# Indirect scatters planned one by one behind a wait on ScalarE or VectorE, and keys times values per head

## The chip, the core and the metric

The kernel runs on one core of a Trainium2 chip. The core has a matrix engine (TensorE, "PE" in the profile; its weight loads are "PEld"), VectorE ("DVE"), ScalarE ("ACT"), GpSimd ("POOL") and SyncE ("SP"). Each takes its own instructions in order and waits for the others on semaphores. Sixteen DMA engines move data between the chip's memory and the core; SP, ACT and POOL can each issue transfers. The metric is the device time of one execution in microseconds (us), given as the median of several runs; lower is better.

## What is computed

A linear attention block is followed by a mixture of eight experts in which each token goes to two of them. Cut to what matters:

```python
# attention: 4 batches, 4 heads, 1088 tokens, head size 32, r = 8
a, b = x @ S1.T, x @ S2.T                 # for queries and for keys
phi = outer(a, b)                         # 64 features a head
kv  = einsum('bhsf,bhsd->bhfd', phi_k, v) # keys times values
z   = phi_k.sum(over tokens)
x   = (phi_q @ kv) / (phi_q @ z + 1e-6)   # 4352 tokens of 128
# router and experts
noisy = x @ w_gate + log1p(exp(x @ w_noise)) * noise
top2, weights = the two largest of 8 and their softmax
out[token] = sum over the two: weight * (relu(x @ w1[e]) @ w2[e])
```

All of it is float32. The hidden size of an expert is 1024.

## The kernel before

The work goes batch by batch through the attention, and in waves through the experts. The tokens of a batch lie in nine chunks: eight of 128 rows, and a last one of 64.

*Attention of a batch* (`keys_values`, L626, and `queries`). VectorE transposes the keys and queries, TensorE multiplies them with the sketch, ScalarE or VectorE copies the result, and VectorE forms the products of features (`features`, L566). POOL copies the values into `vaug` (L629 and L632), a tile with 64 columns a head: 32 of values, one of ones (so that the sum z comes out of the same matmul) and 31 of zeros. TensorE multiplies features by values in L653: per chunk two matmuls, each with two heads side by side as weights (128 columns) and as moving data (128 columns). Only the two blocks on the diagonal, each head with itself, are used. They are copied out to `kvT` and folded with the gate weights (L674). `queries` transposes the query features (L698), multiplies by the folded matrix (L709), and divides.

*Router* (`router`). VectorE and ScalarE find each token's two experts, their weights and a place in the expert's list. For each chunk and each of the two choices POOL then issues one indirect scatter (L794) that writes up to 128 weighted rows from `xg` into the lists `xs` in the chip's memory. The first four chunks of batch 0 are wave 0 (8 scatters), the rest of batch 0 is wave 1 (10), and batches 1 to 3 are waves 2 to 4 (18 each).

*Experts* (`block`). A block is one expert with 128 rows (waves 0, 1 and the last, static one) or 256 rows (waves 2 to 4). Its rows are fetched from `xs` once the scatters of its wave and of the one before have landed. Then TensorE multiplies by w1 (L1054), ScalarE or VectorE applies the relu (L1062 or L1060), TensorE multiplies by w2 (L1069), the result is copied to `y` (L310), and POOL scatters `y` into `pairs` (L794 again), one scatter per 128 rows. Later `sums` reads both rows of every token from `pairs`, adds them and writes the output.

*The order of all this.* A planner written out in the kernel (class `Plan`) takes every piece of work as a job with engines, a cost, a priority and its dependencies. `order` (L92) gives each a planned start by a greedy simulation of the queues, and `write` (L153) emits the instructions in that order; each engine then runs its own in order. Jobs marked `paced` are the scatters of rows from wave 1 on and all the scatters of results. Among the paced ones, the fifth after another may start no sooner than 7.0 us after it (`BURST`, `SPAN`), in planned time. Nothing holds the chip to the planned times: only true dependencies are waited for.

*The memset.* Ahead of each indirect scatter, `pool_scatter` clears one element of a small tile on POOL (L793). Nothing else uses that tile.

Of the kernel before, what the change touches and what calls it, by code (L numbers as in the profile page):

```python
# [8 lines left out]
F32 = mybir.dt.float32  # L9
# [27 lines left out]
class Plan:  # L37
# [4 lines left out]
    RATE = 290e3  # L42
    SLACK = 0.35
    LANES = 8
    BURST, SPAN = 5, 7.0
    SOON = 0.3
    AHEAD = 6.0

# [38 lines left out]
    def order(self):  # L87
        free, done, moved, paced, lanes = {}, [], 0.0, [], []
        left = {j: len(j.deps) for j in self.jobs}
        after = {j: [] for j in self.jobs}  # L90
        for j in self.jobs:
            for d in j.deps:  # L92
                after[d].append(j)
        cand = [j for j in self.jobs if not left[j]]
        number = {j: i for i, j in enumerate(self.jobs)}

        def ready(j, e):

            slack = self.SLACK if e == "PE" else 0.0
            return max((d.end if d.engine == e and d.size is None else d.done + slack for d in j.deps), default=0.0)  # L100

        while cand:
            starts = []
            for j in cand:
                at = 0.0
                for b in j.opens:
                    bufs, _, used = self.tags[b.tag]
                    if b.placed or len(used) < bufs:
                        continue
                    ends = [x.done for x in used[-bufs].users]  # L110
                    if None in ends:
                        at = None
                        break
                    at = max(at, max(ends))
                if at is None:
                    continue
                if j.size is not None:
                    if "SP" in j.engines:
                        at = max(at, moved - self.AHEAD)
                    if "POOL" not in j.engines and len(lanes) >= self.LANES:  # L120
                        at = max(at, lanes[-self.LANES])
                if j.paced and len(paced) >= self.BURST:
                    at = max(at, paced[-self.BURST] + self.SPAN)
                for e in j.engines:
                    starts.append((max(at, free.get(e, 0.0), ready(j, e)), j, e))
            assert starts, [(j.engines, j.prio, [b.tag for b in j.opens]) for j in cand]
            first = min(x[0] for x in starts)
            _, s, _, j, e = min((j.prio, s, number[j], j, e) for s, j, e in starts if s <= first + self.SOON)
            cand.remove(j)
            cost = j.cost[e] if isinstance(j.cost, dict) else j.cost  # L130
            j.start, j.end, j.engine = s, s + cost, e
            free[e] = j.end
            if j.paced:
                paced.append(s)
            j.done = j.end + j.lat + self.SYNC
            if j.size is not None:
                moved = max(moved, j.end + 0.6) + j.size / self.RATE
                j.done = max(j.done, moved + 0.8 if e == "SP" else j.end + 1.4 + 2 * j.size / self.RATE)
                if e != "POOL":
                    lanes.append(j.done)  # L140
            j.opens = [b for b in j.opens if not b.placed]
            for b in j.opens:
                b.placed = True
                self.tags[b.tag][2].append(b)
            done.append(j)
            for a in after[j]:
                left[a] -= 1
                if not left[a]:
                    cand.append(a)
        assert len(done) == len(self.jobs)  # L150
        return done

    def write(self, idle=None):  # L153
        last = 0.0
        for j in self.order():
            if idle is not None and "PE" in j.engine:
                idle(last, j.start)
                last = j.end
            for b in j.opens:
                b.t = self.tags[b.tag][1]()  # L160
            j.emit(j.engine)


@with_exitstack
def kernel(
# [122 lines left out]
    def vec(n):  # L288
        return 0.155 + 0.00104 * n
# [4 lines left out]
    def gps(n):  # L294
        return 0.12 + 0.00092 * n
# [4 lines left out]
    def mm(n):  # L300
        return max(0.205, 0.016 + 0.00162 * n)
# [5 lines left out]
        return {"ACT": act(n), "DVE": vec(n)}  # L307

    def copy(e, o, i):
        A.copy(o, i) if e == "ACT" else V.tensor_copy(o, i)  # L310

    def dma(q, o, i, r, w, prio, size=0, issue=0.45, after=(), done=None):

# [82 lines left out]
    starts = const.tile([P, NW + 1, E], F32, name="starts")  # L396
    stops = const.tile([P, NW, E], F32, name="stops")
    over = const.tile([P, E], F32, name="over")
    vaug = const.tile([P, C + 1, H, 2 * DH], F32, name="vaug")
    phk = const.tile([P, C + 1, H, R * R], F32, name="phk")  # L400
    phq = const.tile([P, C + 1, H, R * R], F32, name="phq")
    kvws = [const.tile([P, 2, 2 * YW], F32, name=f"kvw{i}") for i in range(2)]
# [7 lines left out]
    def pool_job(cost, prio, emit, w, r=()):  # L410
        add("POOL", cost, lambda e: emit(), r=r, w=w, prio=prio)

    def constants():
# [152 lines left out]
    def features(jobs, prio, whole=False, after=(), first=None):  # L566


        ps = new("bank")
# [39 lines left out]
        while i < n:  # L609
            m = i  # L610
            while m < n and m - i < 2 and jobs[m][2] is jobs[i][2]:
                m += 1

            def product(e, i=i, m=m):
                shape = [rows.stop, H * (m - i), R, R]
                V.tensor_tensor(  # L616
                    out=jobs[i][2].t[rows, jobs[i][1]:jobs[m - 1][1] + 1, :, :].rearrange("p c h (i j) -> p (c h) i j", i=R),
                    in0=factors(i, m, 0).unsqueeze(3).to_broadcast(shape),
                    in1=factors(i, m, 1).unsqueeze(2).to_broadcast(shape), op=ALU.mult)
            add("DVE", vec(256 * (m - i)), product, r=list(source), w=[(jobs[i][2], jobs[x][1]) for x in range(i, m)], prio=prio)  # L620
            i = m
        return last

# [2 lines left out]
    def keys_values(b, prio, head=False, after=()):  # L626
        kT, qT, pk, pq, va = new("kT"), new("qT"), new("phk"), new("phq"), new("vaug")
        kld, qld, vld = klds[b], qlds[b], vlds[b]
        pool_job(gps(1024), prio, lambda: G.tensor_copy(  # L629
            va.t[:, 0:C, :, 0:DH].rearrange("p c h d -> p h c d"), vld.t[:, :, 0:C, :]), [(va, 0)],  # L630
            ["ones_v"] + [(vld, l) for l in range(4)])
        pool_job(gps(128), prio, lambda: G.tensor_copy(va.t[0:HB, C, :, 0:DH], vld.t[0:HB, :, C, :]), [(va, 1)],  # L632
                 ["ones_v", (vld, 4), (vld, 5)])
# [13 lines left out]
        for ts in ((0, 1), (2, 3), (4, 5), (6, 7), (8,)) if head else (range(C + 1),):  # L647
            def emit(e, ts=ts):
                for t in ts:
                    K = HB if t == C else P  # L650
                    for a in range(2):
                        hs = slice(2 * a, 2 * a + 2)
                        T.matmul(kvp.t[:, P * a:P * a + P], lhsT=va.t[0:K, t, hs, :].rearrange("p h d -> p (h d)"),  # L653
                                 rhs=pk.t[0:K, t, hs, :].rearrange("p h f -> p (h f)"),
                                 start=(t == 0 and a == 0), stop=(t == C), skip_group_check=True)
            add("PE", 2 * len(ts) * mm(P), emit, lat=0.15, w=[kvp], prio=prio + 3.5,
                r=[(pk, t) for t in ts] + [(va, 0), (va, 1)])
        kvT, kvw = new("kvT"), new("kvw")
        kv_of[b] = (kvw, pq)

        def rows_of(l):
            return slice(64 * l, 64 * l + DH + 1)

        for l in range(2):
            add(EV, either(128), lambda e, l=l: copy(
                e, kvT.t[rows_of(l), :, :],
                kvp.t[rows_of(l), 0:2 * P].rearrange("p (a f) -> p a f", a=2)[:, :, 64 * l:64 * l + 64]),
                r=[kvp], w=[(kvT, l)], prio=prio + 3)
        ps = new("bank")

# [119 lines left out]

    def pool_scatter(**kw):

        G.memset(step[:, 0:1], 0.0)  # L793
        return G.indirect_dma_start(**kw)  # L794

    onehot = {}
# [203 lines left out]
    def block(u, w, e, r, n):  # L1000
# [48 lines left out]
        for g in range(FJ // js):  # L1049
# [7 lines left out]

            def relu(en, hp=hp, h=h):
                if en == "DVE":
                    V.tensor_scalar_max(h.t[:], hp.t[:], 0.0)  # L1060
                else:
                    A.activation(out=h.t[:], in_=hp.t[:], func=AF.Relu)  # L1062
            add(EV, either(512), relu, r=[hp], w=[h], prio=TOP + u)

            def second(_, g=g, h=h):
# [245 lines left out]
```

## Time and profile before

| | us |
|---|---|
| median of 3 runs | 407.78 (405.43 to 415.69) |
| the profiled execution, its own time | 410.3 |
| its span in the trace | 408.5 |
| PE busy / PEld busy | 355.0 / 326.7 |
| POOL busy | 179.9 |
| DVE busy / ACT busy | 153.2 / 137.4 |

The mean clock granted to TensorE over the profiled execution was 0.936 of full speed. The profile lists busy times, a strip of 40 equal slices of the span in which a digit is the busy share in tenths, groups of instructions by line, and who waited for whom. In a row of the timeline stand the start, the duration, the engine, the line, the operation with what it writes and reads, how many instructions are merged, and in brackets the idle time before with what ended it. "issue" means that the profile shows nothing that was waited for, and "remote" that the wait was ended by no instruction of the trace. A matmul in float32 leaves two records. The duration that a record shows overlaps with the next, so the rate is read from starts.

### The profile page before, as it was taken

Reading aid. Unit: us, or ns where it says so; the run is one execution under the profiler, and the core shown is the slowest. Engines: PE = TensorE matmul, PEld = TensorE weight load, DVE = VectorE, ACT = ScalarE, POOL = GpSimd, SP = SyncE. Lnnn points to the kernel's source line nnn. Section 1 sums busy time; section 2 is a strip of 40 time slices with the busy share of each in tenths; the row PEclk is TensorE's granted clock in tenths of the full one; section 3 lists DMA queues with packets and bytes.
Section 4 is the critical chain, followed back from the end, with each engine's and each line's share of the span. In section 5 each row is a group of like instructions: output and inputs, shape, how many; then the busy total and the mean of one; then the engine's idle time right before and its main releaser. Section 6 shows DMA issues by size and latency. Waiting matters only on the chain.

```text
span 408.5 us, 7355 instructions
## 1 busy us (share of the span) xinstructions
PE 355.0 (87%) x2563; PEld 326.7 (80%) x2565; DVE 153.2 (37%) x584; ACT 137.4 (34%) x283; POOL 179.9 (44%) x377
## 2 busy tenths in 40 slices
PE   7989669699998698539999998899999999999960
PEld 4759659599997597529997978799999999999960
DVE  6797638268866379204881000110001110001201
ACT  2253233136423153003533332334333434344320
POOL 7827406641377636850346658124232332324320
PEclk9999898979999979957999999899999999999995
DMA  6999993322511106610142322541121521114503
GB/s 168 275 313 348 247 205 83 100 45 39 116 46 40 42 11 94 102 36 0 19 65 54 64 60 60 126 106 38 36 43 32 156 70 26 34 26 126 144 18 88
DMA packets 66969, 37.80 MB, mean 93 GB/s; under 512 B 48911, under 2 KB 59697, under 8 KB 66928
## 3 DMA queue, kind: packets, MB, share of 16 engines
q1 hardware_dynamic: 61488, 27.33, 29.8%
q0 software_dynamic: 4800, 9.29, 7.0%
q10 hardware_dynamic: 640, 0.67, 0.6%
q8 instruction: 21, 0.34, 0.4%
q14 instruction: 20, 0.16, 0.1%
HBM read 24.24 MB, written 13.29 MB: 92 GB/s over the span
## 4 chain that ended last, share of the span: by engine, by line
issue 37%; POOL 27%; PE 19%; DMA 9%; DVE 5%; POOLq 1%; ACT 1%; SPq 0%; ACTq 0%; DVEq 0%
POOL pairs L794 13%; POOL xs L794 10%; PE acc L1069 5%; PE hp L1054 5%; PE bank L582 3%; DMA ix<-xs 3%; PE bank L653 2%; POOL step L793 2%; DMA vld<-in_v_dram 2%; PE bank L709 2%; DMA x<-in_moe_noise_dram 2%; DMA xs<-xg,to 1%; PE bank L698 1%; DMA pairs<-y,mine 1%; POOL xb L317 1%
## 5 line engine op out<-in xcount | busy, mean ns | idle before, releaser
L1069 PE MATMUL acc<-w2s,h 128*128 128x128 f32 x1152 | 156.1, 281 | 8.7 <-ACT h L1062 8.6
L1069 PEld LDWEIGHTS acc<-w2s,h 128*128 128x128 f32 x1152 | 150.1, 196 | 16.0 <-ACT h L1062 10.7
L1054 PE MATMUL hp<-bT,w1s 128*128 128x128 f32 (+1 forms) x768 | 150.2, 330 | 1.8 <-DVE lim L943 1.8
L794 POOL DMA_INDIRECT pairs<-y,mine x72 | 71.3, 990 | 176.7 <-ACT y L310 153.0
L1062 ACT ACTIVATE h<-hp 128x512 f32<-128x512 f32 x139 | 82.7, 597 | 158.8 <-PE hp L1054 97.8
L1054 PEld LDWEIGHTS hp<-bT,w1s 128*128 128x128 f32 x768 | 113.2, 193 | 8.0 <-issue 2.4
L794 POOL DMA_INDIRECT xs<-xg,to x72 | 71.7, 996 | 27.4 <-issue 21.7
L1044 DVE STREAM_TRANSPOSE bT<-xb 128x256 f32<-128x256 f32 (+1 forms) x40 | 15.6, 390 | 152.0 <-PE hp L1054 95.1
L653 PE MATMUL bank<-phk,vaug 128*128 128x128 f32 (+1 forms) x108 | 17.6, 302 | 11.8 <-issue 11.8
L653 PEld LDWEIGHTS bank<-phk,vaug 128*128 128x128 f32 (+1 forms) x108 | 15.2, 208 | 14.0 <-issue 13.7
L310 ACT COPY y<-acc 128x128 f32<-128x128 f32 (+1 forms) x48 | 15.3, 319 | 31.0 <-PE acc L1069 21.8
L709 PE MATMUL bank<-kvw,pT 128*128 128x98 f32 x144 | 18.9, 276 | 3.7 <-ACT pT L310 3.2
L1102 DVE TENSOR_TENSOR o<-pr 128x512 f32<-128x512 f32 (+2 forms) x12 | 6.8, 567 | 40.5 <-DMA pr<-pairs 38.8
L709 PEld LDWEIGHTS bank<-kvw,pT 128*128 128x128 f32 x144 | 17.5, 192 | 5.2 <-ACT pT L310 3.4
L582 PE MATMUL bank<-sk,kT 128*128 128x128 f32 (+1 forms) x72 | 13.1, 339 | 3.9 <-issue 3.6
L582 PE MATMUL bank<-sk,qT 128*128 128x128 f32 (+1 forms) x72 | 13.6, 327 | 3.2 <-issue 2.1
L310 ACT COPY pT<-bank 128x512 f32<-128x512 f32 (+1 forms) x20 | 10.6, 543 | 15.6 <-PE bank L698 10.2
L582 PEld LDWEIGHTS bank<-sk,kT 128*128 128x128 f32 (+1 forms) x72 | 10.9, 233 | 5.4 <-issue 4.3
L582 PEld LDWEIGHTS bank<-sk,qT 128*128 128x128 f32 (+1 forms) x72 | 11.2, 221 | 4.6 <-issue 3.8
L310 ACT COPY lo<-bank 128x256 f32<-128x256 f32 (+2 forms) x21 | 7.1, 337 | 18.7 <-PE bank L582 14.1
L616 DVE TENSOR_TENSOR phk<-ab 128x512 f32<-128x512 f32 (+1 forms) x20 | 13.2, 680 | 0.3
L793 POOL MEMSET step<- 1x1 f32 x144 | 12.7, 88 | 0.0
(158 smaller groups left out, 247.7 us busy)
## 6 DMA issues: line engine op xcount, KB each, us to landing
w1s<-in_moe_w_dram SPq DMA_DIRECT2D x8, 512.0 KB
w2s<-in_moe_w_dram SPq DMA_DIRECT2D x8, 512.0 KB
xb<-xs SPq DMA_DIRECT2D x96, 32.0 KB
pr<-pairs SPq DMA_DIRECT2D x6, 512.0 KB
kq<-in_k_dram SPq DMA_DIRECT2D x4, 544.0 KB
kq<-in_q_dram SPq DMA_DIRECT2D x4, 544.0 KB
vld<-in_v_dram SPq DMA_DIRECT2D x14, 128.0 KB
out_dram<-o SPq DMA_DIRECT2D x6, 256.0 KB
```

The source lines that it names most:

```text
L310: A.copy(o, i) if e == "ACT" else V.tensor_copy(o, i)
L582: T.matmul(ps.t[rows, 2 * W * i:2 * W * i + 2 * W], lhsT=lhsT, rhs=sk[:].rearrange("p c h x -> p (c h x)"), start=True, stop=True)
L616: V.tensor_tensor(out=jobs[i][2].t[rows, jobs[i][1]:jobs[m - 1][1] + 1, :, :].rearrange("p c h (i j) -> p (c h) i j", i=R), in0=factors(i, ...
L653: T.matmul(kvp.t[:, P * a:P * a + P], lhsT=va.t[0:K, t, hs, :].rearrange("p h d -> p (h d)"), rhs=pk.t[0:K, t, hs, :].rearrange("p h f -> ...
L709: T.matmul(ps2.t[:, c0:c0 + 2 * YW], lhsT=pT.t[:, P * (2 * i + a):P * (2 * i + a) + P], rhs=kvw.t[:, a, :], start=True, stop=True)
L793: G.memset(step[:, 0:1], 0.0)
L794: return G.indirect_dma_start(**kw)
L1044: add("DVE", vec(P * n), lambda _: V.transpose(bT.t[:, 0:P * n], flat()), r=[xb], w=[bT], prio=TOP + u)
L1054: T.matmul(hp.t[:, P * n * i:P * n * (i + 1)], lhsT=w1s[:, e, P * (js * g + i):P * (js * g + i + 1)], rhs=bT.t[:, 0:P * n], start=True, st ...
L1062: A.activation(out=h.t[:], in_=hp.t[:], func=AF.Relu)
L1069: T.matmul(acc.t[:, D * c:D * c + D], lhsT=h.t[:, P * (n * i + c):P * (n * i + c + 1)], rhs=w2s[:, e, j, :], start=(j == 0 and c == 0), st ...
L1102: add("DVE", vec(P * c), lambda e, t=t, o=o, rows=rows, c=c: V.tensor_tensor(out=o.t[rows, 0:c, :], in0=t.t[rows, 0:c, 0, :], in1=t.t[rows ...
```

## The change

There are four parts.

1. *Planned one by one.* `BURST, SPAN = 5, 7.0` becomes `GAP = 1.7`. A paced scatter starts, in planned time, at least 1.7 us after the one before it. The eight scatters of wave 0 are counted among those before, though not held back themselves.
2. *The memset waits.* While writing, `write` notes each single instruction of ACT or DVE with its planned end. For a paced scatter it takes, of those whose planned end is not after the scatter's planned start, the one that ends last (`anchor`), and the memset ahead of the scatter gets a real dependency on it. To make this possible, `copy` and `relu` return their instruction. The unpaced scatters of wave 0 have no such dependency.
3. *Keys times values per head.* `vaug` has 33 columns a head, and the memset of its zeros goes. Each chunk has four matmuls, one a head, with 33 columns of weights and 64 of moving data, where it had two with 128 and 128. The result has 128 columns, where it had 256. The planner's cost a chunk goes from two times `mm(128)`, 0.446, to 0.35.
4. *Copies of the values.* The one copy of eight chunks becomes two, of two heads each; the copy of the last chunk stays. In batch 0 the three run on ACT, in the other batches on POOL as before, with a priority later by 0.5.

The product of features gets a list of engines that holds only DVE and a cost for each of two engines; with that list nothing changes in it.

```diff
-    BURST, SPAN = 5, 7.0
+    GAP = 1.7
...
-                if j.paced and len(paced) >= self.BURST:
-                    at = max(at, paced[-self.BURST] + self.SPAN)
+                if j.paced and paced:
+                    at = max(at, paced[-1] + self.GAP)
...
-            if j.paced:
+            if j.paced or "POOL" in j.engines and j.cost == 1.3:
                 paced.append(s)
...
-        last = 0.0
+        last, seen = 0.0, []
...
-            j.emit(j.engine)
+            self.anchor = max((x for x in seen if x[0] <= j.start), default=(0, 0, None))[2] if j.paced else None
+            ins = j.emit(j.engine)
+            if j.engine in ("ACT", "DVE") and hasattr(ins, "ins"):
+                seen.append((j.end, len(seen), ins))
...
-    vaug = const.tile([P, C + 1, H, 2 * DH], F32, name="vaug")
+    vaug = const.tile([P, C + 1, H, DH + 1], F32, name="vaug")
...
-        pool_job(1.2, 4, lambda: G.memset(vaug[:, :, :, DH:2 * DH], 0.0), ["ones_v"])
...
+        by = ("ACT",) if head else ("POOL",)
...
+        for h in range(0, H, 2):
+            add(by, {"ACT": act(512), "POOL": gps(512)}, lambda e, h=h: v_copy(
+                e, va.t[:, 0:C, h:h + 2, 0:DH].rearrange("p c h d -> p h c d"), vld.t[:, h:h + 2, 0:C, :]),
+                w=[(va, h)], r=["ones_v"] + [(vld, l) for l in range(4)], prio=prio + 0.5)
+        add(by, {"ACT": act(128), "POOL": gps(128)}, lambda e: v_copy(e, va.t[0:HB, C, :, 0:DH], vld.t[0:HB, :, C, :]),
+            w=[(va, 1)], r=["ones_v", (vld, 4), (vld, 5)], prio=prio + 0.5)
...
-                        hs = slice(2 * a, 2 * a + 2)
-                        T.matmul(kvp.t[:, P * a:P * a + P], lhsT=va.t[0:K, t, hs, :].rearrange("p h d -> p (h d)"),
-                                 rhs=pk.t[0:K, t, hs, :].rearrange("p h f -> p (h f)"),
-                                 start=(t == 0 and a == 0), stop=(t == C), skip_group_check=True)
+                        for l in range(2):
+                            T.matmul(kvp.t[64 * l:64 * l + DH + 1, 64 * a:64 * a + 64], lhsT=va.t[0:K, t, 2 * a + l, :],
+                                     rhs=pk.t[0:K, t, 2 * a + l, :],
+                                     start=(t == 0 and a == 0), stop=(t == C), skip_group_check=True)
...
-        G.memset(step[:, 0:1], 0.0)
+        fill = G.memset(step[:, 0:1], 0.0)
+        if plan.anchor is not None:
+            tc.add_manual_dep(fill.ins, plan.anchor.ins.name, DATA, reason="not in a run")
         return G.indirect_dma_start(**kw)
```

More of the change, by code (lines that the diff above doesn't have):

```diff
@@ L309, in copy @@
     def copy(e, o, i):
-        A.copy(o, i) if e == "ACT" else V.tensor_copy(o, i)
+        return A.copy(o, i) if e == "ACT" else V.tensor_copy(o, i)
     def dma(q, o, i, r, w, prio, size=0, issue=0.45, after=(), done=None):
@@ L564, in turned, with features @@
         add("DVE", vec(128 * (c1 - c0) if c0 < C else 64), emit, r=[src], w=[(dst, c0 // 4)], prio=prio)
-    def features(jobs, prio, whole=False, after=(), first=None):
+    def features(jobs, prio, whole=False, after=(), first=None, by=("DVE",)):
         ps = new("bank")
@@ L615, in product @@
                 shape = [rows.stop, H * (m - i), R, R]
-                V.tensor_tensor(
+                (V if e == "DVE" else G).tensor_tensor(
                     out=jobs[i][2].t[rows, jobs[i][1]:jobs[m - 1][1] + 1, :, :].rearrange("p c h (i j) -> p (c h) i j", i=R),
@@ L619, in product @@
                     in1=factors(i, m, 1).unsqueeze(2).to_broadcast(shape), op=ALU.mult)
-            add("DVE", vec(256 * (m - i)), product, r=list(source), w=[(jobs[i][2], jobs[x][1]) for x in range(i, m)], prio=prio)
+            add(by, {"DVE": vec(256 * (m - i)), "POOL": gtt(256 * (m - i))}, product, r=list(source), w=[(jobs[i][2], jobs[x][1]) for x in range(i, m)], prio=prio)
             i = m
@@ L628, in keys_values, with v_copy @@
         kld, qld, vld = klds[b], qlds[b], vlds[b]
[L629 to L633, printed above, removed]
+        by = ("ACT",) if head else ("POOL",)
+        def v_copy(e, o, i):
+            A.copy(o, i) if e == "ACT" else G.tensor_copy(o, i)
+        for h in range(0, H, 2):
[4 more added lines that the diff above has]
+            w=[(va, 1)], r=["ones_v", (vld, 4), (vld, 5)], prio=prio + 0.5)
         turned(kT, kld, 0, 4, prio)
@@ L651, in emit @@
                     for a in range(2):
-                        hs = slice(2 * a, 2 * a + 2)
-                        T.matmul(kvp.t[:, P * a:P * a + P], lhsT=va.t[0:K, t, hs, :].rearrange("p h d -> p (h d)"),
-                                 rhs=pk.t[0:K, t, hs, :].rearrange("p h f -> p (h f)"),
-                                 start=(t == 0 and a == 0), stop=(t == C), skip_group_check=True)
-            add("PE", 2 * len(ts) * mm(P), emit, lat=0.15, w=[kvp], prio=prio + 3.5,
-                r=[(pk, t) for t in ts] + [(va, 0), (va, 1)])
+                        for l in range(2):
+                            T.matmul(kvp.t[64 * l:64 * l + DH + 1, 64 * a:64 * a + 64], lhsT=va.t[0:K, t, 2 * a + l, :],
+                                     rhs=pk.t[0:K, t, 2 * a + l, :],
+                                     start=(t == 0 and a == 0), stop=(t == C), skip_group_check=True)
+            add("PE", 0.35 * len(ts), emit, lat=0.15, w=[kvp], prio=prio + 3.5,
+                r=[(pk, t) for t in ts] + [(va, 0), (va, 2), (va, 1)])
         kvT, kvw = new("kvT"), new("kvw")
@@ L666, in keys_values @@
                 e, kvT.t[rows_of(l), :, :],
-                kvp.t[rows_of(l), 0:2 * P].rearrange("p (a f) -> p a f", a=2)[:, :, 64 * l:64 * l + 64]),
+                kvp.t[rows_of(l), 0:P].rearrange("p (a f) -> p a f", a=2)),
                 r=[kvp], w=[(kvT, l)], prio=prio + 3)
@@ L1059, in relu @@
                 if en == "DVE":
-                    V.tensor_scalar_max(h.t[:], hp.t[:], 0.0)
-                else:
-                    A.activation(out=h.t[:], in_=hp.t[:], func=AF.Relu)
+                    return V.tensor_scalar_max(h.t[:], hp.t[:], 0.0)
+                return A.activation(out=h.t[:], in_=hp.t[:], func=AF.Relu)
             add(EV, either(512), relu, r=[hp], w=[h], prio=TOP + u)
```

## The prediction

> **What bounds the kernel now.** I read the page first (busy times and the 40 slices), then the waits, then the busy time of each engine in chosen stretches, then the timeline of the worst stretch.
>
> ```profile
> span 408.5 us, 7355 instructions
> PE 355.0 (87%) x2563; PEld 326.7 (80%) x2565; DVE 153.2 (37%) x584; ACT 137.4 (34%) x283; POOL 179.9 (44%) x377
> ...
> PE   7989669699998698539999998899999999999960
> ...
> PEclk9999898979999979957999999899999999999995
> ```
>
> PE is busy 87% of the span, so PE sets the time where it is full. Its holes lie in the first half, and the granted clock (the row PEclk) sinks beside or just behind them. The waits say who stood still:
>
> ```profile
> POOL pairs L794 <- ACT y L310: 153.0, 39, 16.9
> ...
> ACT h L1062 <- remote: 33.3, 5, 19.0
> DVE bT L1044 <- remote: 30.1, 3, 16.8
> ```
>
> The 153.0 us of POOL are no loss: a scatter waits for the y that PE and ACT make. The two "remote" rows are odd: ACT and DVE waited up to 19.0 and 16.8 us for no instruction. The stretches (columns: PE, PEld, DVE, ACT, POOL busy with counts, granted clock, DMA share, GB/s) show where:
>
> ```profile
> 31.60:38.90 7.30, 7.05 (x64) 6.81 (x63) 5.98 (x20) 3.08 (x7) 6.21 (x11) 1.00 1.11 347
> ...
> 75.20:82.00 6.80, 3.27 (x12) 2.39 (x12) 2.00 (x5) 0.27 (x2) 4.34 (x8) 0.83 0.40 131
> 82.00:90.00 8.00, 8.00 (x57) 7.67 (x57) 5.20 (x15) 3.22 (x8) 3.14 (x7) 0.72 0.28 49
> ...
> 136.30:140.00 3.70, 0.08 (x1) 0.08 (x1) 0.75 (x3) 0.60 (x1) 3.05 (x7) 1.00 0.17 54
> 140.00:150.00 10.00, 9.33 (x55) 8.90 (x56) 6.08 (x32) 4.67 (x9) 2.36 (x5) 0.66 0.04 10
> ...
> 168.00:182.50 14.50, 4.16 (x13) 2.80 (x12) 0.00 (x0) 0.00 (x0) 9.74 (x20) 0.63 0.28 63
> 182.50:190.00 7.50, 7.50 (x41) 6.73 (x42) 3.30 (x7) 2.05 (x5) 0.00 (x0) 0.57 0.00 0
> 190.00:244.80 54.80, 53.18 (x373) 48.76 (x372) 22.71 (x104) 21.46 (x41) 27.39 (x52) 1.00 0.26 49
> ...
> 254.20:257.00 2.80, 0.01 (x1) 0.02 (x1) 0.00 (x0) 0.60 (x1) 1.57 (x4) 1.00 0.44 66
> 257.00:261.00 4.00, 4.00 (x17) 3.64 (x18) 1.65 (x3) 0.88 (x2) 0.00 (x0) 0.57 0.61 235
> 261.00:393.00 132.00, 132.00 (x964) 125.92 (x964) 12.61 (x33) 52.27 (x99) 40.70 (x77) 1.00 0.28 67
> ```
>
> In each hole POOL alone works, and it works through a run of scatters that wait for nothing. In 168.0 to 182.5 ACT and DVE do nothing at all and PE issues 13 matmul records. The rows 31.60:38.90 and 190.00:244.80 are for comparison: POOL scatters there too, and PE is nearly full. From 261 on, POOL issues as many scatters but most wait for a y: PE is full for all 132 us. The timeline of the worst hole:
>
> ```profile
> 165.08 1.03 PE L1054 MATMUL hp<-bT,w1s 128*128 128x256 f32 x4
> ...
> 167.39 0.96 POOL L794 DMA_INDIRECT xs<-xg,to  x1 [0.22 <-issue]
> ...
> 168.66 0.95 POOL L794 DMA_INDIRECT xs<-xg,to  x1 [0.21 <-issue]
> ...
> 178.75 0.90 POOL L794 DMA_INDIRECT xs<-xg,to  x1 [0.22 <-issue]
> ...
> 182.59 0.60 ACT L1062 ACTIVATE h<-hp 128x512 f32<-128x512 f32 x1 [19.03 <-remote]
> ```
>
> The hp that ACT waits for was done at 166.1; ACT took it at 182.6, after the run's last scatter. PE's gaps are "issue": nothing in the profile holds it. So I read a long run of scatters, one per 1.27 us, as what stalls the other engines. [...]
>
> **The change part by part.**
> *Scatters spaced, the memset waits.* Planned starts of wave scatters move from five per 7.0 us to one per 1.7 us, counting the first wave's eight. Each spaced scatter's memset gets a real wait for the ACT or DVE instruction that the plan ends last before it. When ACT and DVE stand still, POOL now stands still too, so a run breaks itself off. What the holes cost PE, first in idle time. A record of 128 columns takes 0.89/8 = 0.111 us:
>
> ```profile
> 246.99 1.05 PE L1069 MATMUL acc<-w2s,h 128*128 128x128 f32 x8
> 247.88 1.03 PE L1054 MATMUL hp<-bT,w1s 128*128 128x256 f32 x4
> ```
>
> 75.2 to 82.0: 6.8 - 12 x 0.111 = 5.5. 136.3 to 140.0: 3.6. 168.0 to 182.5: 14.5 - 13 x 0.111 = 13.1. 254.2 to 257.0: 2.8. Sum 25.0 us. Then the slow clock behind them, busy time by what is missing from full speed: 8.0 x 0.28 = 2.2; 9.33 x 0.34 = 3.2; 7.5 x 0.43 = 3.2; 4.0 x 0.43 = 1.7. Sum 10.3 us. Together 35.3 us. [...]
>
> The first eight scatters stay without the wait, so what their run costs stays.
>
> *What is late next.* The rows of wave 2, in POOL's timeline and PE's:
>
> ```profile
> 110.79 1.16 POOL L794 DMA_INDIRECT xs<-xg,to  x1 [0.67 <-DVE xg L931]
> ...
> 139.50 0.90 POOL L794 DMA_INDIRECT xs<-xg,to  x1 [0.21 <-issue]
> ...
> 149.17 0.91 POOL L794 DMA_INDIRECT xs<-xg,to  x1 [0.24 <-issue]
> ```
> ```profile
> 159.70 2.98 PE L1054 MATMUL hp<-bT,w1s 128*128 128x256 f32 x12 [1.79 <-DVE lim L943]
> ```
>
> Wave 2's blocks begin 10.5 us after its last scatter. With the first hole gone (5.5 + 2.2 = 7.7) its scatters start at 103.1; 18 of them and 4 result scatters between make 21 gaps of 1.7 = 35.7, so the last starts at 138.8 and the blocks can begin at 149.3. PE, without the first two holes (7.7 + 6.8), gets there at 145.2. So 4.1 us are given back. Behind the waiting memset POOL's queue also holds the copies of v, and SP's queue holds the row fetches, with later loads behind them.
>
> ```profile
> 124.99 1.04 POOL L629 COPY vaug<-vld 128x1024 f32<-128x1024 f32 x1
> ```
> ```profile
> 165.94 1.95 PE L653 MATMUL bank<-phk,vaug 128*128 128x128 f32 x16
> ```
>
> The last batch's copy runs 41 us ahead of its use. That covers it; without the cover PE would wait as long as the copy is late.
>
> At the end the memset no longer lies ahead of the last y: 0.09 for it and 0.21 up to the scatter now come after the copy. Plus 0.3 us.
>
> *A stall that stays.* A wait on a past instruction does not hold POOL where ACT and DVE are ahead of the plan. The trace shows none of the new waits, so: between no stall and all four. I take one the size of the smallest, 2.8 + 1.7 = 4.5 us, because 190 to 244.8, where runs of six scatters or fewer lie between waits, shows PE full but for 1.6 us.
>
> *Keys times values per head.* Per chunk two calls of 128 by 128 columns become four with 33 columns of weights and 64 moving: 4 records become 8. Now 4 x 0.111 = 0.445 us. The nearest row is the fold:
>
> ```profile
> 186.79 0.67 PE L674 MATMUL bank<-wg,kvT 33*64 33x49 f32 x8
> 187.40 1.12 PE L698 MATMUL bank<-ident,phq 128*128 128x128 f32 x4
> ...
> 256.99 1.93 PE L1069 MATMUL acc<-w2s,h 128*128 128x128 f32 x8 [2.80 <-ACT h L1062]
> 258.71 1.91 PE L1054 MATMUL hp<-bT,w1s 128*128 128x256 f32 x4
> ```
>
> It takes 0.61/8 = 0.076 at clock 0.57, where the 128-column record takes 1.72/8 = 0.215; at full clock 0.039 for 49 columns, by 64/49 0.051, so 0.41 a chunk. The 27 chunks of the last three batches then save 27 x 0.035 = 1.0 us. Ends: 0.039 a record (0.31 a chunk) saves 3.6; the 128-column price on each record (0.89) costs 12.0. I take 1.0, by the row nearest in shape. Batch 0's chunks wait for the key features and count nothing.
>
> *Copies of v, the memset of vaug.* In the head two copies leave POOL for three on ACT:
>
> ```profile
> 9.60 1.04 POOL L629 COPY vaug<-vld 128x1024 f32<-128x1024 f32 x1 [0.75 <-DMA vld<-in_v_dram]
> 10.58 0.76 POOL L632 COPY vaug<-vld 64x128 f32<-64x128 f32 x1
> ...
> 16.91 2.19 POOL L372 COPY noise<-x 32x256 f32<-32x256 f32 x6 [0.28 <-DMA x<-in_moe_noise_dram]
> ```
> ```profile
> 9.22 0.37 ACT L310 COPY lo<-bank 128x256 f32<-128x256 f32 x1 [0.52 <-PE bank L582]
> ...
> 11.80 0.41 DVE L601 TENSOR_TENSOR ab<-bank,lo 128x256 f32<-128x256 f32 x1
> ```
>
> POOL waits for the noise transfer at 16.9 in any case, so what it saves there, the memset's time with it, gives nothing. On ACT a second lo copy may come up to 1.2 us later, but DVE takes it only at 11.8: zero, and up to 1.2 if that cover goes.
>
> **The sum.** 408.5 - 35.3 + 4.1 + 0.3 + 4.5 - 1.0 = 381.1 us of span. The profiled run took 410.3 us, 1.8 beyond its span, and lies 2.5 above the median of the runs (407.78): 381.1 + 1.8 - 2.5 = 380.4, said as 380.5.
>
> **The rivals**, each against 407.8.
> The runs of scatters are not the cause. What speaks for it: the releaser is "remote", no row names a shared resource. Against: the heaviest transfers (share 1.11, 31.6 to 38.9) leave PE full, and the holes have shares of 0.17 to 0.44, so load on the transfers is not it. The holes stay: 407.8 + 0.3 - 1.0 = 407, no change.
> Only the long run goes: bursts of more than six still get through where POOL has fallen behind. Gain 13.1 + 3.2 = 16.3: 391.
> All holes go and wave 2's rows come in time: 407.8 - 35.3 + 0.3 - 1.0 = 372.
> The other side: the waits make POOL too slow for PE. One place decides, wave 2's rows: a memset waits for a relu, the relu for PE, and PE runs out of blocks. The gain is used up where the blocks start 35.3 us after 145.2, and slower by over 2% (8.2 us) begins where they start 43.5 us after it: last scatter at 178.2, (178.2 - 103.1)/21 = 3.6 us a scatter. At 4.0 us: 187.1 + 10.5 = 197.6, 52.4 late, 407.8 + 52.4 - 35.3 = 425. For it: POOL's longest wait for a y is 16.9 us, in the rows above. Against: pairs that wait for y already pass at their pace with PE full.
>
> **How the numbers follow.** Forecast (most holes gone) 0.40; only the long run 0.21; all gone 0.12; not the cause 0.14; POOL too slow 0.13. Faster by over 2% (about what a measurement of this kernel tells from no change) 0.73, same 0.14, slower 0.13. Range: from "all gone" with the best matmul price, 407.8 - 35.3 - 3.6 + 0.3 = 369, rounded out to 368, up to "not the cause" and part of the dear matmul price, 412; the slower case stays out. The likeliest's own range is 372 to 391.
>
> **What would show it.** Right: "remote" waits of ACT and DVE fall from 63 us to under 15; no stretch of 3 us with PE idle and POOL busy after 60 us; the granted clock at 1.00 from 82 to 390; POOL's memsets waiting for ACT and DVE; keys times values under 0.42 us a chunk. Wrong: holes of the same length with the scatters spaced (not the cause); or PE idle ahead of the first 256-column matmul, its input waiting for the rows (POOL too slow).

## The result, and the profile after

| | before | after | ratio (95%) |
|---|---|---|---|
| median, us | 409.95 (405.43 to 415.69, 4 runs) | 381.04 (378.53 to 384.15, 4 runs) | 0.9375 (0.9227 to 0.9523) |
| profiled execution / its span, us | 410.3 / 408.5 | 379.21 / 377.5 | |
| mean granted clock | 0.936 | 0.963 | |

The change made the kernel 6.2% faster. One thing has to be said at once, since no later number can be read without it: this holds on the occasion on which it was measured. On three later occasions the kernel before, unchanged, took 367 to 369 us, and the traces taken there, all of other kernels, show no such holes. The changed kernel itself was run on one of the three, and there it was no faster (ratio 1.0091). The experiments tell the two apart; the rest of this section is the measured pair.

The page of the kernel after, the lines that answer to those of before (busy times, then 40 slices):

```profile
span 377.5 us, 7730 instructions
PE 339.0 (90%) x2710; PEld 312.2 (83%) x2712; DVE 152.0 (40%) x586; ACT 139.2 (37%) x284; POOL 181.0 (48%) x377
...
PE   7889767799998999699999999999999999999950
...
PEclk9999998989998999799999999999999999999995
```

The span is 31.0 us shorter: PE is busy 16.0 us less (355.0 to 339.0) and idle 15.0 us less (53.5 to 38.5). PE has more records than before (2710 against 2563) and still less busy time, since less of it runs at the low clock (16.67 us of it against 32.07) and the records of keys times values are short (49 of them without a gap take 1.63 us, from 148.35 on). Behind the first ten slices, the last two left out, the lowest digit of PE is now a 6, where 6, 5 and 3 stood.

The waits of the kernel after (engine, line and what it waited for: us in total, times, longest):

```profile
POOL step L800 <- ACT y L313: 67.3, 27, 4.1
...
ACT h L1070 <- remote: 4.9, 2, 2.7
...
ACT pT L313 <- remote: 3.5, 2, 3.2
...
ACT kvw L313 <- remote: 2.6, 1, 2.6
DVE den L731 <- remote: 2.0, 1, 2.0
...
DVE bT L1053 <- remote: 1.3, 1, 1.3
```

The memsets (L800) now wait for ACT. The "remote" waits of ACT and DVE sum to 14.3 us, where the two rows shown of before held 63.4 and all of theirs 79.3. Its busy times by stretch:

```profile
72.30:76.00 3.70, 1.90 (x24) 1.08 (x25) 0.87 (x3) 0.04 (x1) 2.36 (x4) 1.00 0.56 171
76.33:79.74 3.41, 3.41 (x23) 2.97 (x21) 2.00 (x5) 1.57 (x5) 0.64 (x2) 0.50 0.03 10
...
111.50:116.50 5.00, 3.30 (x73) 2.40 (x72) 3.06 (x7) 0.27 (x1) 3.54 (x6) 1.00 0.14 44
117.29:120.70 3.41, 3.41 (x23) 3.10 (x22) 2.06 (x5) 1.20 (x3) 1.79 (x4) 0.50 0.06 19
...
151.00:155.20 4.20, 1.12 (x15) 0.76 (x13) 1.81 (x4) 0.84 (x3) 3.60 (x8) 0.96 0.24 40
154.84:161.66 6.83, 6.44 (x26) 5.74 (x27) 2.49 (x11) 2.04 (x5) 3.26 (x8) 0.50 0.71 94
...
177.00:361.00 184.00, 183.49 (x1318) 173.74 (x1317) 25.20 (x82) 72.19 (x134) 80.35 (x153) 1.00 0.30 73
```

Small holes stay: 1.8, 1.7 and 3.1 us of idle PE. Behind each the clock falls to 0.50. From start to start a 128-column record of L1063 takes 0.213 us there, against 0.112 at 1.00 (medians of this trace), so I estimate the cost as half of the time that PE is busy in it: (3.41 + 3.41 + 6.44) x 0.50 = 6.6 us. That is 13.2 us in all. From 177 on PE is full. The timeline of the largest one:

```profile
150.87 0.91 POOL L803 DMA_INDIRECT xs<-xg,to  x1 [0.23 <-issue]
...
152.09 0.96 POOL L803 DMA_INDIRECT xs<-xg,to  x1 [0.22 <-issue]
...
153.35 1.34 POOL L803 DMA_INDIRECT xs<-xg,to  x1 [0.22 <-issue]
...
155.18 1.11 PE L705 MATMUL bank<-ident,phq 128*128 128x128 f32 x4 [3.08 <-ACT kvw L313]
...
160.69 1.59 PE L1063 MATMUL hp<-bT,w1s 128*128 128x256 f32 x4
```

It too lies beside a run of scatters, a short one. The last row is PE's first 256-column matmul; no idle time stands ahead of it. The end of the kernel:

```profile
363.94 0.27 ACT L313 COPY y<-acc 128x128 f32<-128x128 f32 x1 [1.25 <-PE acc L1077]
364.32 0.09 POOL L800 MEMSET step<- 1x1 f32 x1 [1.10 <-ACT y L313]
365.05 0.97 POOL L803 DMA_INDIRECT pairs<-y,mine  x1 [0.64 <-issue]
```

The last scatter starts 365.05 - 364.21 = 0.84 us after the copy of its y has ended. The bracket of the scatter says 0.64 between memset and scatter, where unwaited pairs (the rows at 150.87 and after) show 0.22: here a memset that has waited also makes the scatter behind it start about 0.4 us later. Over this whole trace, from the end of the memset to the start of the scatter right behind it, the median is 0.64 us for the 36 memsets that waited over 0.3 us and 0.24 for the other 86.

### The profile page after: what moved, and what is told of

Same layout as the page of the kernel before. It is cut to its first block, busy times and chain, and to the rows that moved or that the text cites. A ratio compares the mean times of both kernels' runs of the same rounds, so it can differ in the third digit from the quotient of the medians.

```text
span 377.5 us, 7730 instructions
## 1 busy us (share of the span) xinstructions
PE 339.0 (90%) x2710; PEld 312.2 (83%) x2712; DVE 152.0 (40%) x586; ACT 139.2 (37%) x284; POOL 181.0 (48%) x377
## 4 chain that ended last, share of the span: by engine, by line
PE 76%; DMA 8%; DVE 7%; issue 3%; POOL 3%; another core or an unknown queue 1%; ACT 1%; SPq 0%; POOLq 0%; DVEq 0%; ACTq 0%
PE hp L1063 32%; PE acc L1077 32%; PE bank L716 4%; PE bank L584 3%; DMA ix<-xs 3%; PE bank L660 2%; PE bank L705 2%; DMA kq<-in_q_dram 2%; POOL xs L803 2%; DMA xs<-xg,to 2%; DVE phk L618 1%; POOL xb L320 1%; PE bank L681 1%; DMA pairs<-y,mine 1%
## 5 line engine op out<-in xcount | busy, mean ns | idle before, releaser
L1077 PEld LDWEIGHTS acc<-w2s,h 128*128 128x128 f32 x1152 | 146.8, 192 | 7.6 <-ACT h L1070 1.8
L1077 PE MATMUL acc<-w2s,h 128*128 128x128 f32 x1152 | 151.8, 276 | 1.3 <-ACT h L1070 0.9
L1063 PE MATMUL hp<-bT,w1s 128*128 128x128 f32 (+1 forms) x768 | 151.3, 333 | 0.9 <-DVE mk L872 0.8
L1063 PEld LDWEIGHTS hp<-bT,w1s 128*128 128x128 f32 x768 | 114.3, 196 | 7.2 <-PE acc L1077 1.0
L800 POOL MEMSET step<- 1x1 f32 x144 | 13.0, 90 | 94.3 <-ACT y L313 67.3
L716 PEld LDWEIGHTS bank<-kvw,pT 128*128 128x128 f32 x144 | 18.8, 207 | 3.5 <-ACT pT L313 3.2
L705 PE MATMUL bank<-ident,phq 128*128 128x128 f32 x72 | 13.1, 318 | 4.1 <-ACT kvw L313 3.1
L705 PEld LDWEIGHTS bank<-ident,phq 128*128 128x128 f32 x72 | 9.7, 165 | 5.1 <-ACT kvw L313 3.3
L660 PE MATMUL bank<-phk,vaug 128*33 128x64 f32 (+1 forms) x216 | 9.5, 221 | 4.1 <-issue 4.1
L1281 PE MATMUL hp<-zb 128*128 128x512 bf16 x38 | 11.1, 430 | 1.6 <-POOL zb L417 1.4
L660 PEld LDWEIGHTS bank<-phk,vaug 128*33 128x33 f32 (+1 forms) x216 | 6.9, 110 | 6.6 <-issue 6.0
L618 DVE TENSOR_TENSOR phq<-ab 128x512 f32<-128x512 f32 (+1 forms) x20 | 12.1, 635 | 0.3
```

The lines of the kernel that those rows point to most:

```text
L618: (V if e == "DVE" else G).tensor_tensor(out=jobs[i][2].t[rows, jobs[i][1]:jobs[m - 1][1] + 1, :, :].rearrange("p c h (i j) -> p (c h) i j ...
L660: T.matmul(kvp.t[64 * l:64 * l + DH + 1, 64 * a:64 * a + 64], lhsT=va.t[0:K, t, 2 * a + l, :], rhs=pk.t[0:K, t, 2 * a + l, :], start=(t == ...
L705: T.transpose(ps.t[:, c0:c0 + P], pq.t[:, t + i, 2 * a:2 * a + 2, :].rearrange("p h f -> p (h f)"), ident[:])
L716: T.matmul(ps2.t[:, c0:c0 + 2 * YW], lhsT=pT.t[:, P * (2 * i + a):P * (2 * i + a) + P], rhs=kvw.t[:, a, :], start=True, stop=True)
L800: fill = G.memset(step[:, 0:1], 0.0)
L1063: T.matmul(hp.t[:, P * n * i:P * n * (i + 1)], lhsT=w1s[:, e, P * (js * g + i):P * (js * g + i + 1)], rhs=bT.t[:, 0:P * n], start=True, st ...
```

## The experiments

The theory at the start: a long run of indirect scatters stalls the other engines, and the wait breaks the runs. The rival: the planned spacing does it, or the values do. Each ratio is to the kernel before, run beside it. The four occasions are named B to E here (the result above is A); A and D are those with holes. The traces of B to E are of the kernels that were run there; of the kernel before there is a trace on A alone.

| occasion | kernel before, us | holes in the traces |
|---|---|---|
| A (the result) | 409.95 | yes |
| B (e1 to e4) | 369.09 | no |
| C (e5 to e8) | 367.36 | no |
| D (e9, e10), same chip as B | 406.19 | yes |
| E (e11, e12) | 369.42 | no |

### The change without the wait

```diff
         fill = G.memset(step[:, 0:1], 0.0)
-        if plan.anchor is not None:
-            tc.add_manual_dep(fill.ins, plan.anchor.ins.name, DATA, reason="not in a run")
```

> The changed kernel with its planned order, only the dependency of the memset taken out. Theory (the real waits break the runs up): POOL falls behind the plan and catches up in runs, holes of 3 us and more with PE idle come back, 395 us or more. Rival (the order planned at 1.7 us is enough): 379 to 385 us, no holes, PE busy as in the changed kernel.

Measured: 369.94 us, ratio 1.0042 (1.0008 to 1.0075). Neither level came, since the kernel before took 369.09 beside it: nothing was there to be saved.

### The wait alone, and the planned gap alone

Both are edits of the kernel before. The first adds part 2 of the change, with the old plan and the old values:

```diff
...
-        G.memset(step[:, 0:1], 0.0)
+        fill = G.memset(step[:, 0:1], 0.0)
+        if plan.anchor is not None:
+            tc.add_manual_dep(fill.ins, plan.anchor.ins.name, DATA, reason="not in a run")
```

> The kernel before with nothing but the waits of the memset added; bursts of five planned as before, keys times values as before. Theory: the holes at 75, 136, 168 and 254 us go, 382 to 392 us. Rival (the planned spacing does it): 403 us or more, since the planned order is the old one.

The second adds part 1:

```diff
-    BURST, SPAN = 5, 7.0
+    GAP = 1.7
...
-                if j.paced and len(paced) >= self.BURST:
-                    at = max(at, paced[-self.BURST] + self.SPAN)
+                if j.paced and paced:
+                    at = max(at, paced[-1] + self.GAP)
...
-            if j.paced:
+            if j.paced or "POOL" in j.engines and j.cost == 1.3:
```

> The kernel before with nothing but the plan changed, one scatter per 1.7 us, and no waits. Theory: real runs form again, 395 to 410 us, with ACT and DVE idle over 5 us at a stretch. Rival (planned spacing does it): 380 to 388 us.

Measured: the wait alone 370.36, ratio 1.0044 (1.001 to 1.0078); the gap alone 368.84, ratio 0.9987 (0.9949 to 1.0025). Both levels were missed for the same reason. What follows is small: without holes the wait costs 1 us or so, and the gap with the old values nothing.

### Keys times values and the copies alone

Parts 3 and 4 on the kernel before, with the old plan and no wait:

```diff
...
-                        T.matmul(kvp.t[:, P * a:P * a + P], lhsT=va.t[0:K, t, hs, :].rearrange("p h d -> p (h d)"),
...
+                        for l in range(2):
+                            T.matmul(kvp.t[64 * l:64 * l + DH + 1, 64 * a:64 * a + 64], lhsT=va.t[0:K, t, 2 * a + l, :],
...
-            add("PE", 2 * len(ts) * mm(P), emit, lat=0.15, w=[kvp], prio=prio + 3.5,
+            add("PE", 0.35 * len(ts), emit, lat=0.15, w=[kvp], prio=prio + 3.5,
...
```

> The kernel before with the old plan rule and no waits, but keys times values per head and the copies of the values split. Theory: the holes stay, 403 to 409 us, a chunk of keys times values takes 0.25 to 0.42 us. Rival (fewer and shorter matmuls in the hole are what helped): below 395 us.

Measured: 361.19, ratio 0.9798 (0.9727 to 0.9869), a gain of 7.9 us where I had forecast 1.0. The time lies below the 395 of the rival, but with the kernel before at 369.09 beside it neither theory nor rival was tested on the holes. The price of a batch's keys times values can be read where PE runs on without a gap, first with the old values (the wait alone), then with the new ones (this kernel):

```profile
149.74 4.37 PE L656 MATMUL bank<-phk,vaug 128*128 128x128 f32 x36
154.04 1.16 PE L585 MATMUL bank<-sk,qT 128*128 128x128 f32 x8
```
```profile
142.15 2.33 PE L660 MATMUL bank<-phk,vaug 128*33 128x64 f32 x72
144.41 1.16 PE L584 MATMUL bank<-sk,qT 128*128 128x128 f32 x8
```

From start to start nine chunks take 4.30 us before and 2.26 after: 0.478 and 0.251 a chunk, 0.119 and 0.0314 a record. The new chunk lies at the low end of what was expected for this run. Over all 36 chunks that is 36 x 0.227 = 8.2 us; over the 27 that I had counted it would be 6.1. The measured 7.9 is nearer to all 36.

### Four kernels on another occasion

The changed kernel itself, and the values alone once more, have no new edit. The kernel before without any pacing of scatters:

```diff
-                if j.paced and len(paced) >= self.BURST:
-                    at = max(at, paced[-self.BURST] + self.SPAN)
```

"Values and waits" is the change with the old pacing:

```diff
-    GAP = 1.7
+    BURST, SPAN = 5, 7.0
...
-                if j.paced and paced:
-                    at = max(at, paced[-1] + self.GAP)
+                if j.paced and len(paced) >= self.BURST:
+                    at = max(at, paced[-self.BURST] + self.SPAN)
...
-            if j.paced or "POOL" in j.engines and j.cost == 1.3:
+            if j.paced:
```

> The changed kernel as it is, beside the kernel before on one chip. Theory A (the holes hang on the chip as well as on the runs of scatters; the earlier chip had them): where the kernel before shows no holes and takes about 369 us, the change gives no gain, 368 to 374 us; where it takes about 408 us, 378 to 385 us. Rival B (the gain is the change's own on every chip): a ratio near 0.94 whatever the kernel before takes.

> The kernel before without any pacing in the plan and without waits, so the runs of scatters get as long as the data allows. Theory A on a chip without holes: within 1% of the kernel before, PE full through runs of 15 and more; on a chip with holes: 10 us or more over it. Rival (a run of scatters alone always stalls the other engines): longer than before by 10 us or more on any chip.

> The changed kernel with the old rule of five scatters per 7.0 us in the plan; waits and keys times values per head stay. If the rule of 1.7 us is what costs the 9 us by which the changed order without waits was slower than the values part alone: 360 to 365 us on a chip where the kernel before takes 369. If the waits cost as much by themselves: 366 us or more. On a chip with holes: 372 to 385 us.

> The kernel before with keys times values per head and split copies of the values only, once more, in the same call as the changed kernel. On a chip without holes 359 to 363 us, the fastest of the four, since neither the waits nor the 1.7 us pace buys anything there. On a chip with holes 395 us or more, as the runs are not broken up.

| kernel | us | ratio (95%) |
|---|---|---|
| the change | 369.8 | 1.0091 (1.0057 to 1.0126) |
| no pacing | 366.57 | 0.9948 (0.9908 to 0.9987) |
| values and waits | 360.52 | 0.9834 (0.9788 to 0.9879) |
| values only | 359.69 | 0.9805 (0.9779 to 0.983) |

All four lie where they were expected for a chip without holes. That the holes hang on the chip is not borne out: the chip of B, which had shown none, showed them on D.

The kernel without pacing has the longest runs of scatters of all. Its three longest (16, 17 and 22 scatters less than 1.6 us apart), by stretch:

```profile
114.30:133.40 19.10, 19.10 (x171) 18.40 (x170) 14.82 (x76) 9.73 (x20) 15.73 (x31) 1.00 0.16 51
147.30:167.70 20.40, 20.40 (x165) 19.06 (x164) 13.35 (x44) 7.94 (x16) 16.80 (x32) 1.00 0.32 73
178.30:205.70 27.40, 27.40 (x189) 25.78 (x188) 5.67 (x20) 10.72 (x20) 22.28 (x43) 1.00 0.30 67
```

PE is full through all of them at clock 1.00, with POOL at 15.7 to 22.3 us busy. So these runs of scatters, by themselves, stalled nothing on C.

The change and "values and waits" differ in the planned gap alone, and in 9.3 us. The place in the timeline of the change (the last scatter of wave 2, the first use of the fetched rows on DVE, and PE's first 256-column matmul):

```profile
139.61 1.01 POOL L803 DMA_INDIRECT xs<-xg,to  x1 [0.24 <-issue]
...
146.33 0.21 DVE L1005 COPY_PREDICATED mine<-holds,ix 128x16 uint32<-128x16 uint32 x1 [3.70 <-DMA ix<-xs]
...
148.22 2.07 PE L1063 MATMUL hp<-bT,w1s 128*128 128x256 f32 x4 [3.24 <-DVE den L731]
```

The stretch of the change in which the clock was low there:

```profile
146.76:157.00 10.24, 8.05 (x28) 6.92 (x29) 4.88 (x17) 2.15 (x4) 3.75 (x8) 0.50 0.58 94
```

The same three rows in the timeline of "values and waits":

```profile
129.17 0.89 POOL L803 DMA_INDIRECT xs<-xg,to  x1 [0.22 <-issue]
...
135.15 0.20 DVE L1005 COPY_PREDICATED mine<-holds,ix 128x16 uint32<-128x16 uint32 x1 [1.20 <-DMA ix<-xs]
...
137.05 2.98 PE L1063 MATMUL hp<-bT,w1s 128*128 128x256 f32 x12 [1.17 <-DVE bT L1053]
```

With the gap of 1.7 the 18 scatters of wave 2 take 41.0 us (98.65 to 139.61), with the old rule 29.0 (100.16 to 129.17). DVE then stands 3.70 us waiting for the rows, with the division of batch 3's attention (`den`) behind that wait in its queue, and PE stands 3.24 us behind `den`. PE loses these 3.2 us of idle time and 0.7 more behind them, and at the clock of 0.50 half of its 8.05 busy us, 4.0. At the same place "values and waits" loses 1.2 us of idle time and nothing to the clock, so the place accounts for 3.2 + 0.7 + 4.0 - 1.2 = 6.7 of the 9.3. The change without the wait has the same late rows (18 scatters in 41.5 us, DVE waiting 3.38), so it is the plan, not the wait. With the old values the gap costs nothing; in that trace PE's first 256-column matmul, at 153.84, has no idle time ahead of it. That it has other work left when the rows come, since keys times values take it longer, would explain this; no run takes it apart.

### The gap at 1.4, and the values alone where holes occur

```diff
-    GAP = 1.7
+    GAP = 1.4
```

> The changed kernel with a planned gap of 1.4 us in place of 1.7; waits and values part stay. Theory (on a chip without holes the changed order loses its gain where PE idles for wave 2's late rows at about 145 us): rows come some 6 us earlier (21 gaps less 0.3 each), the idle of PE there shrinks below 1 us, 360 to 364 us where the kernel before takes 368. Rival (the order is worse for another reason): 367 us or more, same idle. On a chip with holes: 375 to 385 us.

> The values part alone with the old plan and without waits, beside the run above. On a chip without holes 359 to 363 us. On a chip where the kernel before takes about 408 us: if runs of scatters are needed for the holes there, 390 us or more and over 15 us longer than the run above; if the holes have nothing to do with them, within 8 us of it.

Here the kernel before took 406.19, so the holes were back, on the chip of occasion B. Measured: gap 1.4, 393.63 (392.05 to 400.85), ratio 0.9684 (0.9612 to 0.9757); values only, 411.91 (two runs), ratio 1.0148 (1.0055 to 1.0241). The 393.63 is the median of four runs, three of them at 392.05 to 394.33. The 411.91 lies where it was expected if runs of scatters are needed for the holes. The very kernel that gained 2% on B and C loses 1.5% on D. PE by slices on its page of occasion D:

```profile
PE   8888958499985789734999999999999999999960
```

Its worst hole, by stretch:

```profile
172.30:179.50 7.20, 2.62 (x31) 1.50 (x27) 0.00 (x0) 0.00 (x0) 6.07 (x11) 0.80 0.63 116
179.50:189.90 10.40, 2.38 (x9) 1.77 (x8) 0.03 (x1) 0.32 (x2) 6.39 (x14) 0.50 0.15 44
```

The timeline of that hole:

```profile
172.09 0.45 PE L660 MATMUL bank<-phk,vaug 128*33 128x64 f32 x9 [0.37 <-issue]
...
172.90 0.32 PE L660 MATMUL bank<-phk,vaug 128*33 128x64 f32 x4 [0.36 <-issue]
...
173.66 0.32 PE L660 MATMUL bank<-phk,vaug 128*33 128x64 f32 x4 [0.45 <-issue]
...
174.42 0.35 PE L660 MATMUL bank<-phk,vaug 128*33 128x64 f32 x5 [0.43 <-issue]
...
189.58 0.26 ACT L313 COPY kvT<-bank 33x128 f32<-33x128 f32 x1 [19.70 <-remote]
```

The hole lies in a run of 12 scatters 1.27 us apart (172.32 to 186.23). PE passes a few records every 0.75 us or so, held by nothing the profile shows, and ACT and DVE do nothing; ACT's wait of 19.70 us is a "remote" one. The same program on occasion B ran through a longer run, of 22 (133.40 to 160.84), with PE busy for 26.06 of its 27.44 us and for all of its last part:

```profile
147.00:162.00 15.00, 15.00 (x115) 14.25 (x115) 12.17 (x43) 7.63 (x14) 12.39 (x24) 1.00 0.35 74
```

The kernel with the gap of 1.4, on occasion D, has smaller holes. One of 3.77 us lies beside four scatters 1.3 to 1.5 us apart (113.96 to 117.96), one of 2.89 in a run of six. By stretch, and the second in its timeline:

```profile
116.30:120.10 3.80, 0.04 (x1) 0.04 (x1) 0.06 (x1) 0.35 (x2) 2.18 (x5) 0.73 0.16 52
...
149.10:155.60 6.50, 3.22 (x32) 2.51 (x34) 5.63 (x17) 1.15 (x4) 5.23 (x10) 1.00 0.68 95
```
```profile
154.12 1.10 PE L1063 MATMUL hp<-bT,w1s 128*128 128x256 f32 x4 [2.89 <-issue]
```

So where holes occur at all, parts 1 and 2 do save: 411.91 to 393.63 on one occasion, 18.3 us, between two kernels that differ in these parts alone (with the gap at 1.4). With the runs broken up PE's longest standstill behind 63 us falls from 6.78 to 3.77 us. A hole does not need a long run, though, since one stays beside four scatters; and the planned order of the other engines changes along with the gap, which no run separates. The expected 375 to 385 for the gap of 1.4 was missed, and what it does to wave 2's late rows without holes was not seen. That 1.7 saves more than 1.4 is likely (381.04 on A, against 393.63 on D) but was not measured on one occasion.

### Two of the kernels on a fifth occasion

> Values part and waits under the old rule of five scatters per 7.0 us, for the occasion on which the kernel before takes about 406 us. Theory (what counts is that POOL halts when ACT and DVE halt, whatever the planned pace): 380 to 395 us, no stretch over 4 us with PE idle beside a run of scatters. Rival (the planned gap is what spreads the scatters): 400 us or more, like the values part alone. If the kernel before takes about 369 us on this occasion: 359 to 364 us.

> The changed kernel without the waits, for the occasion on which the kernel before takes about 406 us. Theory (waits count): runs of seven and more form and stall PE, ACT and DVE, 395 us or more. Rival (planned gap counts): 376 to 386 us, as with the waits. If the kernel before takes about 369 us on this occasion: 367 to 373 us.

The occasion had no holes (before: 369.42). Values and waits 360.67, ratio 0.9759 (0.9719 to 0.9799); the change without the wait 370.02, ratio 0.9991 (0.9952 to 1.003). Both as on C and B. Whether the wait or the planned gap broke up the runs on occasion A therefore stays open: neither part ran by itself where holes were.

## Why the prediction came out

The median came out 0.5 us from the forecast (381.04 against 380.5), by the outcome that I had put first: most holes gone. The closeness is luck. The span was forecast at 381.1 us and measured 377.5. I then took off 2.5 us because the profiled execution of before lay that far above its median; that of after lay 1.8 below its own. Term by term:

- **The holes, -35.3.** That fewer scatters in a row mean less standing still is borne out where holes occur: values with runs 411.91, the runs broken up 393.63. The reading behind it went too far. "A long run of scatters is what stalls the other engines" is refuted as a general statement by the runs of 16 to 22 at a full PE. A run stalls only on some occasions, for a cause outside the kernel: the same program with the values alone took 361.19 on B and 411.91 on D. The rival "not the cause" falls on D, and its 407 us on A; it would have been right on B, C and E, in that the holes do not come from scatters alone.
- **A stall that stays, 4.5.** Three small holes and the slow clock behind each: 13.2, three times what I took.
- **What is late next, 4.1.** I counted 35.7 us for the 18 scatters; they took 46.5 on A (104.42 to 150.87) and 41.0 on C. On C it was the right place (wave 2's rows, then DVE, then PE) and too small: the price of the gap was 9.3. On A no such wait shows: PE's first 256-column matmul, at 160.69, has no idle time ahead of it. I had not seen that DVE's queue holds batch 3's attention behind the wait for the rows, nor that the stop also lowers the clock.
- **Keys times values, -1.0.** The step that failed in size: 0.41 a chunk forecast, 0.251 measured, below even my best end (0.31). On A itself 49 of its records without a gap take 1.63 us (148.35 to 149.98), 0.27 a chunk. I took the fold's price by its columns. The batch that I counted at nothing seems to count as well. Without holes the term is 7.9 and 7.7 us.
- **The memset after the last y, 0.3.** Measured 0.84 - 0.27 = 0.57: the wait also delays the scatter behind the memset.
- **The waits as such** cost 0 to 1 us without holes (1.0044 alone; 360.52 against 359.69). "POOL too slow" through waits did not happen; the planner's gap is what made rows late.

Errors thus cancelled. The two traces of A show by how much. The clock was 0.50 from 45.55 to 48.96, 62.62 to 66.03, 79.68 to 86.51, 141.12 to 147.95, 171.84 to 188.91 and 257.18 to 260.59 before, and from 62.68 to 66.09 and in the three stretches shown above after; half of PE's busy time in them is my estimate of what it cost.

| PE on A, us | before | after | difference |
|---|---|---|---|
| idle | 53.53 | 38.50 | -15.03 |
| lost to the slow clock (busy there 32.07 and 16.67) | 16.04 | 8.34 | -7.70 |
| the rest of its busy time | 338.93 | 330.66 | -8.27 |

Idle time and clock gave 22.7 us where the sum had 35.3 - 4.1 - 0.3 - 4.5 = 26.4, and the rest of the busy time fell by about what the new matmuls give without holes (7.7 and 7.9) where the sum had 1.0. The ends of matmuls are modelled in the profile, so the last row is the least sure.

Without holes, the kernels of C lead from the kernel before to the change one part at a time: -7.7 for the values, +0.8 for the waits, +9.3 for the gap, together +2.4. These are differences along one chain, so they must add up and prove nothing. The parts do not simply add: on B the gap alone, with the old values, came out 0.25 us faster and the wait alone 1.27 us slower than the kernel before.

Of the signs named: "remote" waits under 15, right (14.3). No stretch of 3 us with PE idle and POOL busy, missed by one of 3.08. The clock at 1.00 from 82 on, wrong (0.50 from 117.29 to 120.70 and from 154.84 to 161.66). Memsets waiting for ACT and DVE, right. Keys times values under 0.42, right, by far.

On best versions: without holes "values only" (359.69 and 361.19) and "values and waits" (360.52, 360.67) beat both the kernel before and the change. With holes "values only" is slower than the kernel before (two runs), and the change is the fastest that was measured, on A. "Values and waits" was not measured with holes.

## What to carry to other kernels

Before explaining an idle time that no instruction accounts for, run the unchanged kernel again on another occasion: here it took 406 or 369 us on one and the same chip, and a cause that comes and goes decides what a change is worth. The pacing rule that kept a queue from bursting here also delayed its last member (18 scatters in 41.0 us, in 29.0 by the rule of five per 7.0 us), and what waited for that member held DVE's whole queue for 3.70 us; look there first. Price a matmul of a new shape by a run of records without gaps, not by scaling a neighbour's columns: that gave 0.41 us a chunk here, where 0.251 was measured.

## What the runs showed of the hardware

Traces with holes are also traces with losses. The number of semaphore events that each trace holds, and its "remote" waits:

```
kernel, occasion          instructions  semaphore events  remote waits, us
before, A                         7355              5460              81.1
after, A                          7730              5587              14.3
gap 1.4, D                        7728              5797              10.7
values only, D                    7648              5484              33.7
values only, B (same program)     7648              8089                 0
the change, C                     7730              8105                 0
the other eight, B C E       7350-7730         8111-8131                 0
```

Between 28 and 33% of the events are missing exactly on A and D. Where they go missing can be read from the two traces of "values only", counted up to the same scatters. Up to the first one, at 30 us, both hold about as many (653 on B, 642 on D); from there to the 109th, at 228 and 278 us, 4926 and 2697; from there to the end 2510 and 2145. So the losses begin with the scatters. They go on where no hole is left: from the 73rd scatter to the 109th (211 to 278 us on D) the traces hold 1553 and 796, and there PE is busy for 64.68 of the 67.40 us on D. "Remote" then means here that the event which ended the wait was not recorded. That ACT took hp 16 us late stands by the two recorded times, but what held it until then the trace has lost. Whether the losses and the holes have one cause no run shows, since each was recorded alike; the cause of both stays open.

The price of narrow weights was the other surprise: 0.0314 us a record with 33 weight columns and 64 moving ones, against 0.119 with 128 and 128, a quarter of the time for half the moving columns. The new matmuls also have fewer weight columns, and the two heads of a pair write to different partitions, 0 to 32 and 64 to 96; which of these makes the price, no run took apart.

The clock fell here without a full standstill. In all fourteen traces it changes in steps of 3.41 us; in the trace of before on A it stays at 0.50 for 3.41, 3.41, 6.83, 6.83, 17.07 and 3.41 us up to 261 us. PE in the step ahead of a fall, first in the change's trace on C, then in the trace of after on A:

```profile
143.35:146.76 3.41, 1.63 (x15) 1.39 (x14) 0.39 (x3) 0.59 (x1) 2.79 (x8) 1.00 0.76 90
```
```profile
113.88:117.29 3.41, 2.13 (x31) 1.54 (x27) 1.01 (x3) 0.26 (x1) 1.89 (x4) 1.00 0.12 39
```

On C the clock fell 1.8 us into a standstill that began at 144.98, with PE busy for 48% of the step; on A it fell with PE busy for 62%. Over the 1364 steps at full clock of all traces, the clock fell after each of the 29 with PE busy for 45% or less, and after none of the 1298 with PE busy for more than 63%; between the two it went either way. In the two traces of A, 204 of these steps, it fell after each of the 10 with PE busy for 42% or less, after two of the nine between 45 and 63%, and after none of the other 185.
